# Transposing the normalised attention output by the DMA crossbar instead of by TensorE, per head pair

## The chip, the cores and the metric

The kernel runs on one NeuronCore of a Trainium2 chip. The core has a matmul engine (TensorE, PE in the profile, with its weight loads listed as PEld), a vector engine (VectorE, DVE), an activation engine (ScalarE, ACT), GpSimd (POOL) and a queue engine (SyncE, SP). POOL and SP issue the DMA transfers of this kernel. The metric is the device time of one launch in microseconds. The profile comes from one execution; its times count from the first instruction.

## The reference

Block-sparse attention over 4 batches, 8 heads, 768 positions and a head size of 64, and then a gated feed-forward network (FFN) over the 3072 tokens:

```
scores = (1/8) * q @ k.T                 # per batch and head, 768 x 768
scores = where(mask, scores, -1e9)       # blocks of 32: neighbours, first, last, 3 sampled per row block
attn   = softmax(scores)
x      = (attn @ v), heads side by side  # 3072 x 512
gate   = sigmoid(x @ w_gate);  val = x @ w_val      # 512 -> 1536
out    = (gate * val) @ w_out                       # 1536 -> 512
```

## The kernel before

The work is cut into twelve units, a batch and a third of its queries (256 positions) each; three units make a batch. In a unit the eight heads go as four head pairs, called pair 0 to pair 3. For a pair, three steps of score matmuls (`qk`, L406) fill two PSUM score buffers in turn, ACT takes the exponential (L416), DVE multiplies by the mask (L422), and 24 matmuls (`pv`, L445) form the attention output with one extra column for the softmax sum. `norm` (L453 to L462) takes the reciprocal of that column and multiplies, and writes the tile `x16`: 128 positions in partitions, two halves of 128 features.

The FFN wants features in partitions, so x must be turned into x^T. `turn` (L464) does this by two TensorE transposes per pair into PSUM (L466), and `evac` (L472) copies the result into the tile `xT` on DVE (through L227) or ACT (L225). When all four pairs of a unit are in `xT`, the unit's FFN can start: twelve blocks of eight matmuls (L532), each followed by a tanh on ACT (L543) and a gate on DVE (L548), and at last two output projections of twelve matmuls (`y`, L571), whose results go out by a store from SP's queue (L589).

Two units overlap. In the slots of unit n, the FFN of unit n-1 runs, and in the first two slots the output projections of unit n-2. The values of pair 3 of unit n-1 come in slot 0 of unit n, and the FFN of unit n-1 begins in slot 2.

For batches 1 to 3, q and k are already transposed by the DMA crossbar in the kernel before: one transfer for k and one for q per batch on SP's queue (L375), each of 24 blocks of 128x128. For batch 1, DVE first pairs the heads up (L364). For batches 2 and 3, POOL loads the pairs directly (L622). Batch 0 is transposed on TensorE.

The order of the work on every engine is fixed before the launch by a planner in the kernel, the class `Plan`. Each task has costs in microseconds per engine, dependencies, sometimes a due time, and a lag until its successors may start. The planner runs through time, gives each free engine the first ready task of its list, and so writes one order per engine. The engines then follow that order and wait for each other by semaphores. A DMA task has a lag that stands for its landing: 10 us for the q and k transposes, 55 us for the loads of batches 2 and 3. SP takes its transfers strictly in the written order.

Of the kernel before, what the change touches and what calls it, by code (L numbers as in the profile page):

```python
# [13 lines left out]
f16 = mybir.dt.float16  # L14
# [6 lines left out]
B, H, S, D = 4, 8, 768, 64  # L21
# [3 lines left out]
NP = H // 2  # L25
# [5 lines left out]
UQ = 256  # L31
NU = S // UQ
PE, ACT, DVE, DMA = "PE", "ACT", "DVE", "DMA"
DMA_RATE = 0.385
XB, PB, VB = 4, 4, 5
# [86 lines left out]
def kernel(  # L122
# [11 lines left out]
    nc = tc.nc  # L134
# [6 lines left out]
            name=nc.get_next_instruction_name(), act_func_set_id=_set_id  # L141
# [12 lines left out]
    work = ctx.enter_context(tc.tile_pool(name="work", bufs=1))  # L154
# [90 lines left out]
    plan = Plan({'m': 4, 's': 2})  # L245
# [4 lines left out]
    used = {nm: [] for nm in ("pr", "P", "x16", "th", "ht", "xT")}  # L250

    def ring(nm, bufs):

        i = len(used[nm]) - bufs
        return [used[nm][i]] if i >= 0 else []
# [115 lines left out]
    def xbar(src, dst, b, deps):  # L371


        def go(eng):
            nc.sync.dma_start_transpose(  # L375
                dst[b % 2].rearrange("a p (t n) -> a (p t) n", n=128),
                src.rearrange("a p t h d -> a (p t h d)"),
            )

        return plan.add([(DMA, 0.01)], go, deps, lag=10.0)  # L380
# [48 lines left out]
    class Pair:  # L429
# [23 lines left out]
        def norm(self, eng):  # L453
            rz = work.tile([128, 2, 2, 1], f32, tag="rz", bufs=3, name="rz")
            nc.vector.reciprocal(rz, self.acc[:, :, :, D : D + 1])  # L455
            self.x16 = work.tile([128, 2, 2, D], f16, tag="x16", bufs=4, name="x16")
            nc.vector.tensor_tensor(  # L457
                self.x16,
                self.acc[:, :, :, 0:D],
                rz.broadcast_to([128, 2, 2, D]),  # L460
                op=ALU.mult,
            )  # L462
# [16 lines left out]
        def value(self):  # L479
            a = plan.add([(PE, 0.8)], self.pv, self.products + [vdone[self.b, self.p]],  # L480
                         take=[self.bank])
            used["P"].append(a)
            read["pv", self.b, self.p] = [a]
            self.normed = plan.add([(DVE, 0.6)], self.norm, [a] + ring("x16", 4),
                                   free=[self.bank])

        def xt(self):
            c = plan.add([(PE, 0.12)], self.turn, [self.normed], take=[self.bank2])
            used["x16"].append(c)
            deps = [used["xT"][self.n - XB]] if self.n >= XB else []  # L490
            xdone[self.n].append(
                plan.add([(DVE, 0.29), (ACT, 0.37)], self.evac, [c] + deps,
                         free=[self.bank2])
            )
# [107 lines left out]
    xTs = [[] for _ in units]  # L602
    xdone = [[] for _ in units]
# [171 lines left out]
```

The softmax here doesn't subtract the row's maximum and nothing guards it: scores larger than these inputs give would overflow.

## Time and profile before

| | |
|---|---|
| median of 8 runs | 306.28 us (305.92 to 307.78) |
| the profiled execution | 306.2 us, its span 304.4 us |
| granted TensorE clock | 0.997 |
| PE, DVE, ACT busy | 96%, 66%, 69% of the span |
| transposes of x on PE (L466) | 96, in 48 pairs |
| evacuations of x^T | 31 on DVE (mean 292 ns), 17 on ACT (mean 372 ns) |
| SP's transfers | 24 stores, 6 transposes of q and k, 4 loads of constants |

A row of the groups names line, engine, operation and tiles, then the count, the total busy time, the mean duration, and the idle time of the engine before it with what ended it. Matmul durations overlap, so the place a matmul takes is read from start to start. A row of the timeline has its start and length in microseconds. A row of SP's timeline shows how long the queue was held by issuing the transfer, or by the waits between merged ones, and not when the data landed; the median time to landing stands in the list of DMA issues.

### The profile page before, as it was taken

Reading aid. Unit: us, or ns where it says so; the run is one execution under the profiler, and the core shown is the slowest. Engines: PE = TensorE matmul, PEld = TensorE weight load, DVE = VectorE, ACT = ScalarE, POOL = GpSimd, SP = SyncE. Lnnn points to the kernel's source line nnn. Section 1 sums busy time; section 2 is a strip of 40 time slices with the busy share of each in tenths; the row PEclk is TensorE's granted clock in tenths of the full one; section 3 lists DMA queues with packets and bytes.
Section 4 is the critical chain, followed back from the end, with each engine's and each line's share of the span. In section 5 each row is a group of like instructions: output and inputs, shape, how many; then the busy total and the mean of one; then the engine's idle time right before and its main releaser. Section 6 shows DMA issues by size and latency. Waiting matters only on the chain.

```text
span 304.4 us, 7858 instructions
## 1 busy us (share of the span) xinstructions
PE 291.5 (96%) x3326; PEld 209.7 (69%) x3326; DVE 201.0 (66%) x474; ACT 210.7 (69%) x340; POOL 48.5 (16%) x65
## 2 busy tenths in 40 slices
PE   3978999999999999999999999999999999999994
PEld 1354785786786786786686686687687687687771
DVE  4769878876676678676676577576576577576240
ACT  3669986776776776776776776776776776774431
POOL 8943000584000059200000000000000000000000
PEclk9999999999999999999999999999999999999998
DMA  7999999999500699930100480100100100100101
GB/s 100 179 202 202 206 204 185 234 160 129 121 1 2 158 151 128 156 71 2 71 2 0 129 152 1 71 2 2 69 2 2 69 2 4 69 2 2 69 2 70
DMA packets 62768, 25.75 MB, mean 85 GB/s; under 512 B 45812, under 2 KB 59660, under 8 KB 62732
## 3 DMA queue, kind: packets, MB, share of 16 engines
q0 software_dynamic: 40400, 14.16, 40.9%
q1 hardware_dynamic: 22332, 11.09, 14.7%
q8 instruction: 26, 0.43, 0.6%
q14 instruction: 10, 0.08, 0.1%
HBM read 28.39 MB, written 6.29 MB: 114 GB/s over the span
## 4 chain that ended last, share of the span: by engine, by line
PE 92%; ACT 2%; DMA 2%; POOL 1%; DVE 1%; issue 1%; DVEq 0%; POOLq 0%
PE m L532 42%; PE m L571 21%; PE m L445 13%; PE s L406 13%; DMA k<-in_k_dram 2%; PE m L466 2%; ACT pt L416 1%; PE m L338 1%; ACT mask L225 1%; POOL k L178 1%; POOL q L178 0%; POOL v L178 0%; DVE pt L422 0%; DVE kT L227 0%; PE m L303 0%
## 5 line engine op out<-in xcount | busy, mean ns | idle before, releaser
L416 ACT ACTIVATE pt<-s 128x1024 f16<-128x1024 f32 x144 | 140.2, 1027 | 4.5 <-PE s L406 3.7
L422 DVE TENSOR_TENSOR pt<-pt,mask 128x1024 f16<-128x1024 f16 x144 | 97.2, 687 | 38.9 <-ACT pt L416 38.5
L532 PE MATMUL m<-xT,wg 128*128 128x256 f16 x576 | 86.7, 273 | 0.0
L532 PE MATMUL m<-xT,wv 128*128 128x256 f16 x576 | 86.4, 273 | 0.0
L543 ACT ACTIVATE th<-m 128x256 f32<-128x256 f32 x144 | 54.6, 390 | 43.9 <-PE m L532 36.6
L548 DVE SCALAR_TENSOR_TENSOR ht<-th,m 128x256 f16<-128x256 f32 x144 | 57.3, 417 | 16.2 <-ACT th L543 14.8
L571 PE MATMUL m<-wo,ht 128*128 128x512 f16 x288 | 66.0, 379 | 0.0
L532 PEld LDWEIGHTS <-wv 128*128 128x128 f16 x576 | 56.4, 98 | 6.5
L532 PEld LDWEIGHTS <-wg 128*128 128x128 f16 x576 | 51.3, 98 | 12.5 <-issue 7.2
L445 PE MATMUL m<-vex,pt 128*128 128x65 f16 x1152 | 46.5, 196 | 1.8 <-ACT mask L225 1.6
L445 PEld LDWEIGHTS <-pt 128*128 128x128 f16 x1152 | 42.6, 99 | 7.6 <-issue 5.3
L571 PEld LDWEIGHTS <-ht 128*128 128x128 f16 x288 | 26.6, 98 | 30.7 <-issue 2.1
L406 PE MATMUL s<-qT,kT 64*128 64x256 f16 x576 | 47.1, 279 | 0.6 <-DVE qT L227 0.3
L582 ACT ACTIVATE ysb<-m 128x512 f32<-128x512 f32 x24 | 14.3, 597 | 35.3 <-PE m L571 35.3
L406 PEld LDWEIGHTS <-kT 64*128 64x128 f16 x576 | 22.0, 95 | 15.8 <-issue 8.6
L622 POOL DMA_DIRECT2D kp<-in_k_dram x16 | 13.0, 820 | 63.9 <-DMA kT<-kp 38.2
L455 DVE RECIPROCAL rz<-m 128x4 f32<-128x4 f32 x48 | 8.7, 182 | 19.5 <-PE m L445 18.9
L457 DVE TENSOR_TENSOR x<-m,rz 128x256 f16<-128x256 f32 x48 | 20.4, 425 | 1.7
L227 DVE COPY xT<-m 128x256 f16<-128x256 f16 x31 | 9.0, 292 | 10.9 <-PE m L466 10.9
L466 PE MATMUL m<-ident,x 128*128 128x128 f16 x96 | 13.3, 221 | 0.1
L622 POOL DMA_DIRECT2D qp<-in_q_dram x16 | 13.1, 823 | 1.2 <-DMA kp<-in_k_dram 0.9
L466 PEld LDWEIGHTS <-x 128*128 128x128 f16 x96 | 9.0, 99 | 6.1 <-DVE x L457 0.7
(36 smaller groups left out, 73.2 us busy)
## 6 DMA issues: line engine op xcount, KB each, us to landing
out_dram<-ysb SPq DMA_DIRECT2D x24, 256.0 KB, 2.0
v<-in_v_dram POOLq DMA_DIRECT2D x3, 768.0 KB, 11.1
wg<-in_moe_w_gate_dram POOLq DMA_DIRECT2D x4, 384.0 KB, 12.7
wv<-in_moe_w_val_dram POOLq DMA_DIRECT2D x4, 384.0 KB, 13.7
wo<-in_moe_w_out_dram POOLq DMA_DIRECT2D x3, 512.0 KB, 16.9
kp<-in_k_dram POOLq DMA_DIRECT2D x16, 96.0 KB, 4.7
qp<-in_q_dram POOLq DMA_DIRECT2D x16, 96.0 KB, 4.4
k<-in_k_dram POOLq DMA_DIRECT2D x4, 192.0 KB, 5.4
```

The costliest lines, as they stand in the source:

```text
L406: nc.tensor.matmul(score[self.bank.slot][:, a, i, :], kT[b % 2][o : o + D, p, t * 128 : (t + 1) * 128], qT[b % 2][o : o + D, p, u * UQ : ( ...
L416: nc.scalar.activation(self.pt, score[self.bank.slot], AF.Exp, bias=0.0, scale=SCALE)
L422: nc.vector.tensor_tensor(self.pt, self.pt, m.unsqueeze(1).broadcast_to([128, 2, 2, UQ]), op=ALU.mult,)
L445: nc.tensor.matmul(self.acc[:, s, a, :], self.steps[t // 2].pt[:, a, t % 2, s * 128 : (s + 1) * 128], vex[self.b % 2][:, 2 * self.p + a, t ...
L457: nc.vector.tensor_tensor(self.x16, self.acc[:, :, :, 0:D], rz.broadcast_to([128, 2, 2, D]), op=ALU.mult,)
L466: nc.tensor.transpose(m16(self.bank2.slot)[:, s * 128 : (s + 1) * 128], self.x16[:, s, :, :], ident,)
L532: nc.tensor.matmul(pg[:, i, :], w[:, c, f * 128 : (f + 1) * 128], xTs[self.n][0][:, c, :], start=(c == 0), stop=(c == 3),)
L543: nc.scalar.activation(th, spare[bank.slot][:, 0:UQ], AF.Tanh, bias=0.0, scale=0.5)
L548: nc.vector.scalar_tensor_tensor(self.ht[:, f, :], in0=box[0], scalar=1.0, in1=spare[bank.slot][:, UQ : 2 * UQ], op0=ALU.add, op1=ALU.mult,)
L571: nc.tensor.matmul(spare[bank.slot], self.ht[:, f, s * 128 : (s + 1) * 128], wo[:, f, :], start=(f == 0), stop=(f == NF - 1),)
L582: nc.scalar.activation(ysb, spare[bank.slot], AF.Copy, bias=0.0, scale=0.5)
L622: nc.gpsimd.dma_start(dst[:, p, :, a, :], src[b, 2 * p + a].rearrange("(n t) d -> n t d", t=NT),)
```

## The change

For units 1 to 11, the two transposes on TensorE and the copy out of PSUM are replaced by one crossbar transfer per head pair, issued from SP's queue: `x16` (128 x 256) goes as two 128x128 blocks straight into the pair's place in `xT`. The planner gives it 0.05 us of its DMA resource and a lag of 3.0 us. The ring of `x16` tiles grows from four to six, as a tile is now held until its transfer has read it. Unit 0 keeps the TensorE path. The transposes of q and k stay as they were.

```diff
         def norm(self, eng):
...
-            self.x16 = work.tile([128, 2, 2, D], f16, tag="x16", bufs=4, name="x16")
+            self.x16 = work.tile([128, 2, 2, D], f16, tag="x16", bufs=6, name="x16")
...
-            self.normed = plan.add([(DVE, 0.6)], self.norm, [a] + ring("x16", 4),
+            self.normed = plan.add([(DVE, 0.6)], self.norm, [a] + ring("x16", 6),
                                    free=[self.bank])
 
+        def xbar(self, eng):
+            if not xTs[self.n]:
+                xTs[self.n].append(
+                    work.tile([128, NP, UQ], f16, tag="xT", bufs=XB, name="xT")
+                )
+            nc.sync.dma_start_transpose(
+                xTs[self.n][0][:, self.p, :].rearrange("a (s n) -> a s n", s=2),
+                self.x16.rearrange("a s h d -> a (s h d)"),
+            )
+
         def xt(self):
+            if self.n > 0:
+                deps = [used["xT"][self.n - XB]] if self.n >= XB else []
+                c = plan.add([(DMA, 0.05)], self.xbar, [self.normed] + deps, lag=3.0)
+                used["x16"].append(c)
+                xdone[self.n].append(c)
+                return
             c = plan.add([(PE, 0.12)], self.turn, [self.normed], take=[self.bank2])
```

## The prediction

> **What bounds the kernel now.** I read the engine shares and the slices first, then the chain, then a window of one unit, then the timeline of PE, and last the queue of SP, which takes on the new work.
>
> ```profile
> PE 291.5 (96%) x3326; PEld 209.7 (69%) x3326; DVE 201.0 (66%) x474; ACT 210.7 (69%) x340; POOL 48.5 (16%) x65
> ...
> PE 92%; ACT 2%; DMA 2%; POOL 1%; DVE 1%; issue 1%; DVEq 0%; POOLq 0%
> ...
> L457 DVE TENSOR_TENSOR x<-m,rz 128x256 f16<-128x256 f32 x48 | 20.4, 425 | 1.7
> L227 DVE COPY xT<-m 128x256 f16<-128x256 f16 x31 | 9.0, 292 | 10.9 <-PE m L466 10.9
> L466 PE MATMUL m<-ident,x 128*128 128x128 f16 x96 | 13.3, 221 | 0.1
> ...
> out_dram<-ysb SPq DMA_DIRECT2D x24, 256.0 KB, 2.0
> ...
> kT<-kp SPq DMA_TRANSPOSE x3, 7.2
> qT<-qp SPq DMA_TRANSPOSE x3, 5.7
> ```
>
> PE is the bound and almost the whole chain. DVE and ACT have 30% to spare. The window of one whole unit (columns: PE, PEld, DVE, ACT, POOL busy, then granted clock) confirms it: PE is busy from end to end at full clock, and from 36 to 300 us the wait view has no row for PE's matmuls.
>
> ```profile
> 148.32:171.40 23.08, 23.08 (x277) 16.95 (x274) 15.44 (x35) 16.78 (x28) 0.00 (x0) 1.00 0.07 25
> ```
>
> So what leaves PE is gained in full, and whatever PE waits for is lost in full. The timeline of PE (start, length) shows what a pair of transposes costs in place, first without one, then with one:
>
> ```profile
> 150.56 0.60 PE L532 MATMUL m<-xT,wv 128*128 128x256 f16 x4
> 151.09 0.28 PE L406 MATMUL s<-qT,kT 64*128 64x256 f16 x2
> ...
> 157.98 0.60 PE L532 MATMUL m<-xT,wv 128*128 128x256 f16 x4
> 158.42 0.27 PE L466 MATMUL m<-ident,x 128*128 128x128 f16 x2
> 158.63 0.50 PE L406 MATMUL s<-qT,kT 64*128 64x256 f16 x6
> ```
>
> From the FFN's four to the scores is 0.53 us without and 0.65 us with the transposes. Durations of 221 ns overlap; scores after an FFN or output matmul pay a switch of about 0.1 us, which the shorter transposes partly cover. Unrounded start times give 0.112 us for a pair of transposes in front of scores, and 0.111 in front of an output projection.
>
> **Part 1: transposes leave PE.** 44 head pairs (units 1 to 11), 0.112 us each: 4.9 us off PE, 0.45 us per unit. All of it lies on the path. The 44 PSUM evacuations (0.29 us on DVE or 0.37 on ACT) lie beside PE; they are worth nothing, and should PE not be the bound they would be 1.5 us per unit at most. The deeper ring of x16 and the PSUM slots that come free cost nothing; the wait of norm on the sixth last crossbar transfer is over by then, as six pairs are one and a half units, 34 us.
>
> The Trainium skill, page "VectorE: DVE Perf Modes", section "The three transpose paths", puts a 128x128 transpose at 390 ns on TensorE and 1309 ns by the crossbar, and its rules advise TensorE where PSUM will do, which speaks against this change. By its figures the sum would be 88 x 0.39 = 34 us off PE and a transfer of 2.6 us; the trace's 0.112 us for two decides.
>
> **Part 2: 44 crossbar transfers on SP's queue.** No row shows one of two blocks. The rows of 24 blocks: SP is held 3.58 to 4.25 us (5.62 once, under loads), about 0.15 us a block, and landing follows the end of issue by 1.5 to 3.6 us (5.50 minus 3.58, 6.12 minus 3.96, 5.74 minus 4.25, 7.24 minus 3.65). A plain store holds SP 0.33 us and lands after 2.0 us, 5.8 to 7.5 us while batch loads run. So one transfer takes 0.33 plus 1.5 to 3.6, or 1.8 to 3.9 us; I take 2.3, near the quiet rows. The ends are 1.8 and 7.8 (the slowest row of 24 blocks). SP's total, 44 x 0.4 = 18 us, is no bound.
>
> What waits: the FFN of a unit needs all four pairs, and the last, pair 3, has least time. From the end of its norm to the first FFN matmul the timeline gives 6.63 us in seven units, 5.15 in units 1 and 7, 4.43 in unit 4, 4.45 in unit 11; between them lie pair 0's values, two scores and two output projections. With two transposes gone from that stretch, 0.22 less: 4.2 us at the worst. 2.3 us fits, and so does 3.9. The new waits on PE's queue (at most four semaphores at 51 ns, 11 times) run ahead of the matmuls: the one of scores at 68.41 us was over 1.9 us before they began.
>
> **Part 3: the queue in front of it.** SP issues in order:
>
> ```profile
> 48.57 5.62 SPq L375 DMA_TRANSPOSE kT<-kp  x1
> 54.24 0.58 SPq L589 DMA_DIRECT2D out_dram<-ysb  x1
> 54.87 4.04 SPq L375 DMA_TRANSPOSE qT<-qp  x1
> 58.95 0.63 SPq L589 DMA_DIRECT2D out_dram<-ysb  x1
> ```
>
> The store at 54.24 had its data at 52.04 (the ysb row of ACT) and stood 2.2 us behind kT; the next was ready at 55.27 and stood 3.7 us behind qT. A pair 3 caught there keeps PE waiting. Three places:
>
> Unit 1: norm ends 50.85, inside kT's issue. Issue at 54.2, landing 56.5; the FFN would start at 56.01 less four pairs, 55.56. Loss 1.0 us. Its ends: 0 if it goes first; 7.6 us if qT goes first too (that lands at 62.65, plus some 0.5).
>
> Units 4 and 7: kT and qT of batches 2 and 3 are entered when the planner's clock says so, at 10 plus 55 us of its lags after the last batch's qT, however early the data land. Its costs for a unit are 12 x 0.88 + 2 x 2.6 + 6 x 0.54 + 4 x 0.8 = 22.20 us without transposes, where the trace has 23.09. So 65.02 planned us are 67.6 of the trace's: from 52.3 (q's pair copies, started at 50.77 and worth 1.5) plus 0.25 (two transposes gone before a fixed due time) to 120.2, then 187.8. Norms of pairs 2 and 3 end at 115.48 and 120.85 in unit 4, at 186.62 and 189.41 in unit 7. Both marks fall between, 0.7 and 1.6 us ahead of pair 3, which is no more than this reckoning's error. If caught: SP has nothing else to wait for, issues kT and qT after pair 2, and is free after 0.4 + 3.65 + 0.3 + 4.25 (unit 4) or 0.4 + 3.96 + 0.3 + 3.58 (unit 7), at 124.1 and 194.9. Landing 126.4 and 197.2 against FFN starts of 125.07 and 194.35: 1.3 and 2.8 us. Lower ends 0; upper ends 1.6 us more by the 3.9.
>
> In unit 4, POOL's batch loads follow kT's landing (38.2 us of POOL's wait is on it) and come 6 to 18 us later than before; batch 3 is used 70 us on, so that costs nothing. Output stores queued behind cost nothing either: four ysb buffers, and the last store has no crossbar near.
>
> **The sum.** The profiled execution took 306.2 us (span 304.4 and 1.8 around it), 0.1 under the median. 306.2 - 4.9 + 1.0 + 2.0 (one of the two later places, near the mean of 1.3 and 2.8) = 304.3; on the median, 304.4.
>
> **Rivals.** *Caught in neither later place:* DVE has fewer copies, so norm may come earlier than its old place behind v's copies; against it, both marks lie ahead of pair 3. 306.3 - 4.9 + 1.0 = 302.4, 301.4 without unit 1's loss.
>
> *Caught in both:* 306.3 - 4.9 + 1.0 + 1.3 + 2.8 = 306.5, no difference. For it: both marks fall inside; against: one error shifts both.
>
> *Slower, by latency:* a two-block transfer takes as long to land as one of 24. It decides at 5.8 us, where units 1, 4, 7 and 11 lose 0.9 + 1.6 + 0.9 + 1.6 = 5.0 us. At kT's 7.2 us the seven other units lose 0.8 each and these 2.3, 3.0, 2.3, 3.0: 16 us, 317. For it: no landing under 5.5 in the transposes' rows, and 7.5 for a store under loads; against: issue grows with blocks, and the stores' 2.0.
>
> *Slower, by order:* in unit 1 qT enters before pair 3, 7.6 us in place of 1.0, about 309 to 311. Against: DVE's order has norm (50.22) just before q's copies (50.77), qT needs the last of four, and norm only moves earlier.
>
> **How the numbers follow.** Forecast 0.38; neither 0.20; both 0.20; latency 0.11; order 0.06; 0.05 for a rearranged plan that loses more. Measurement can tell about 0.2%, 0.6 us. The forecast's own range is 303 to 306. Low is the neither case without unit 1's loss, 301.4; high takes in both with slower landing (306.5 plus 1.6), 308.1; what is left out is most of latency and order. Faster: 0.36 of the forecast, 0.20, 0.04 of both, 0.02 of a mild latency: 0.62. Same: 0.11 of both, 0.02 and 0.01: 0.14. Slower: 0.24.
>
> **What would show it.** Right: no transpose on L466 after unit 0; units without kT and qT at 22.64 us with PE full; two-block transfers landing in about 2.3 us; a PE wait on xT's DMA only at the FFN's start in units 1 and 4 or 7, with the transfer's issue late behind qT. Wrong: a PE wait at every unit's FFN (latency), units still at 23.09 (the pair costs less than 0.112 once gone), or one wait of 5 us or more in unit 1 (order).

## The result, and the profile after

The changed kernel is slower by about 1%: 309.49 us median of 11 runs (307.09 to 310.42) against 306.42 us for the kernel before in 32 runs. The ratio on record, which is not that of the two medians (1.0100), is 1.0081, 95% interval 1.0062 to 1.0101. The forecast was 304.4 us. The profiled execution took 308.3 us, its span is 306.5 us.

The page's rows that answer to those of before:

```profile
PE 288.6 (94%) x3238; PEld 202.7 (66%) x3238; DVE 192.4 (63%) x444; ACT 205.9 (67%) x326; POOL 48.5 (16%) x65
...
PE   3978999699999999999999999699999999999995
...
PEclk9999999999999999999999999899999999999999
...
PE 76%; DMA 18%; POOL 2%; issue 1%; ACT 1%; DVE 0%; POOLq 0%
...
L548 PE MATMUL m<-xT,wg 128*128 128x256 f16 x576 | 87.8, 274 | 5.3 <-DMA xT<-x 5.3
```

The rows of slices of before:

```profile
PE   3978999999999999999999999999999999999994
...
PEclk9999999999999999999999999999999999999998
```

PE has less to do, as intended: 88 transposes and their weight loads are gone. But PE's row of slices, which was full from unit 1 to the end, has two notches (a 6 in the eighth and in the 26th slice). DMA has gone from 2% to 18% of the chain: 4% are transfers of x^T, and most of the rest are the first loads, to which the profile follows the chain back from unit 1's wait. (It links them by copies on DVE that end as the late transfer is issued; the rows of SP's queue below show what held that transfer.) And the FFN's first matmuls, L548 in the new file, have 5.3 us of idle time in front of them, in three waits that each end with a crossbar transfer. The granted clock has a notch too, in the slice of PE's second one.

The starts of the units' FFNs say where the time went. In the quiet units, from one FFN to the next is 22.64 us (103.62, 126.27, 148.92, 171.56, 194.20), where before it was 23.09. That is the 0.45 us that four pairs of transposes were to save. Three stretches are longer: from unit 1's FFN to unit 2's 25.23 us (2.6 too many), from unit 2's to unit 3's 23.25 (0.6), from unit 7's to unit 8's 26.81 (4.2). The timeline of PE at units 1 and 7 (start, length, idle before and what ended it):

```profile
55.14 0.50 PE L548 MATMUL m<-xT,wg 128*128 128x256 f16 x3
58.07 0.27 PE L548 MATMUL m<-xT,wg 128*128 128x256 f16 x1 [2.42 <-DMA xT<-x]
...
194.20 0.50 PE L548 MATMUL m<-xT,wg 128*128 128x256 f16 x3
197.14 0.36 PE L548 MATMUL m<-xT,wg 128*128 128x256 f16 x1 [2.44 <-DMA xT<-x]
```

Three matmuls run, on pairs 0 to 2; the fourth needs pair 3 and waits. From the first start to the fourth are 2.93 and 2.94 us, where three matmuls take 0.33: 2.6 us lost each time. SP's queue at the same places shows why:

```profile
46.38 1.17 SPq L492 DMA_TRANSPOSE xT<-x  x1
48.72 6.92 SPq L375 DMA_TRANSPOSE kT<-kp  x1
55.76 1.18 SPq L492 DMA_TRANSPOSE xT<-x  x1
...
185.43 1.38 SPq L492 DMA_TRANSPOSE xT<-x  x1
187.16 3.60 SPq L375 DMA_TRANSPOSE kT<-kp  x1
191.06 3.63 SPq L375 DMA_TRANSPOSE qT<-qp  x1
194.79 1.20 SPq L492 DMA_TRANSPOSE xT<-x  x1
```

Pair 3's norm had ended at 51.00 and 188.57 us, but its transfer was issued at 55.76 and 194.79, when SP came free of k, and of k and q. Once issued it landed in 2.27 us in unit 1, and PE went on 2.35 us after the issue in unit 7. The columns of the next view are PE, PEld, DVE, ACT and POOL busy, and then the granted clock; the two windows are unit 7's wait and the time just after it:

```profile
194.20:197.20 3.00, 0.56 (x6) 0.36 (x5) 0.69 (x1) 1.99 (x3) 0.00 (x0) 1.00 0.79 155
197.20:200.60 3.40, 3.40 (x35) 2.78 (x35) 0.85 (x3) 0.38 (x1) 0.00 (x0) 0.50 0.42 151
```

After the wait, PE works for 3.4 us at half clock. The 24 value matmuls that take 0.78 us elsewhere took 1.34 us there. That is the rest of what unit 7 lost, 4.2 us: 2.6 of waiting and 1.6 for the clock. After unit 1's wait the clock did not fall in this execution.

The books close to 0.1 us. Up to the last copy of the output out of PSUM (300.08 before, 302.87 after) the trace is 2.8 us longer: minus 4.9 for 44 pairs, plus 2.6 (unit 1), 0.6 (unit 2), 2.6 and 1.6 (unit 7), and 0.4 by which unit 0's FFN started later (31.64 against 31.27), before the change has begun to act. From that copy to the end of the span are 3.66 us, 0.7 less than the 4.35 of before; the traces of the other runs with 44 transfers have 3.65 to 3.69, and no run here shows why.

### The profile page after: what moved, and what is told of

Its sections match the earlier page's. It is cut to its first block, busy times and chain, and to the rows that moved or that the text cites. A ratio compares the mean times of both kernels' runs of the same rounds, so it can differ in the third digit from the quotient of the medians.

```text
span 306.5 us, 7750 instructions
## 1 busy us (share of the span) xinstructions
PE 288.6 (94%) x3238; PEld 202.7 (66%) x3238; DVE 192.4 (63%) x444; ACT 205.9 (67%) x326; POOL 48.5 (16%) x65
## 4 chain that ended last, share of the span: by engine, by line
PE 76%; DMA 18%; POOL 2%; issue 1%; ACT 1%; DVE 0%; POOLq 0%
PE m L548 39%; PE m L587 17%; PE m L445 11%; DMA v<-in_v_dram 10%; PE s L406 10%; DMA wv<-in_moe_w_val_dram 5%; DMA xT<-x 4%; POOL q L178 1%; POOL k L178 0%; POOL wv L188 0%; POOL wg L188 0%; ACT ysb L598 0%; POOL v L178 0%; DVE vex L384 0%; ACT pt L416 0%
## 5 line engine op out<-in xcount | busy, mean ns | idle before, releaser
L548 PE MATMUL m<-xT,wg 128*128 128x256 f16 x576 | 87.8, 274 | 5.3 <-DMA xT<-x 5.3
L548 PE MATMUL m<-xT,wv 128*128 128x256 f16 x576 | 87.0, 274 | 0.0
L564 DVE SCALAR_TENSOR_TENSOR ht<-th,m 128x256 f16<-128x256 f32 x144 | 56.5, 417 | 20.2 <-ACT th L559 19.9
L548 PEld LDWEIGHTS <-wv 128*128 128x128 f16 x576 | 56.6, 98 | 12.6 <-issue 5.8
L548 PEld LDWEIGHTS <-wg 128*128 128x128 f16 x576 | 50.6, 98 | 14.5 <-issue 9.3
L445 PEld LDWEIGHTS <-pt 128*128 128x128 f16 x1152 | 44.1, 100 | 5.8 <-issue 4.7
L384 DVE COPY vex<-v 128x768 f16<-128x768 f16 x16 | 5.1, 369 | 3.3 <-DMA v<-in_v_dram 3.3
L338 PE MATMUL m<-ident,pr 128*128 128x128 f16 x48 | 5.8, 276 | 0.7 <-DVE pr L329 0.4
L338 PEld LDWEIGHTS <-pr 128*128 128x128 f16 x48 | 4.1, 125 | 3.0 <-DVE pr L329 1.7
```

What stands on the lines that cost most here:

```text
L338: nc.tensor.transpose(m16(bank.slot)[:, (t - t0) * 128 : (t - t0 + 1) * 128], box[0][:, t, :, :], ident,)
L445: nc.tensor.matmul(self.acc[:, s, a, :], self.steps[t // 2].pt[:, a, t % 2, s * 128 : (s + 1) * 128], vex[self.b % 2][:, 2 * self.p + a, t ...
L548: nc.tensor.matmul(pg[:, i, :], w[:, c, f * 128 : (f + 1) * 128], xTs[self.n][0][:, c, :], start=(c == 0), stop=(c == 3),)
L564: nc.vector.scalar_tensor_tensor(self.ht[:, f, :], in0=box[0], scalar=1.0, in1=spare[bank.slot][:, UQ : 2 * UQ], op0=ALU.add, op1=ALU.mult,)
```

## The experiments

The theory after the result: pair 3's transfer stands on SP's queue behind the long transposes of k and q, in units 1 and 7; PE waits 2.6 us each time, and such a wait can drop the clock to half for 3.4 us. The first rival: small crossbar transfers are slow among other DMA traffic wherever they stand, or SP's traffic slows PE. The second, on the clock: it has another cause than PE's idleness.

### Unit 1's place in the queue alone

The planner gets a due time for k's and q's transposes of batch 1 (and a smaller lag, which keeps the places of batches 2 and 3 where they were). PE's order is that of the changed kernel.

```
-        return plan.add([(DMA, 0.01)], go, deps, lag=10.0)
+        return plan.add([(DMA, 0.01)], go, deps, at=52.0 if b == 1 else 0.0, lag=10.0)
...
-                lag=55.0,
+                lag=54.2,
```

> Only unit 1's queue order changes: the crossbar transfer of k for batch 1 gets a due time of 52 us in the plan, so that pair 3 of unit 1 stands in front of it on SP's queue; all other entries of SP's queue keep their places and PE's order is the same to the last instruction. Queue theory: the wait of 2.6 us before unit 1's FFN goes (at most 0.3 us is left), the one of unit 7 stays at 2.6 us, and the time falls by 2.6 us, or by up to 4.3 us where the clock had dropped after it: 305.2 to 307.0 against 309.5 for the changed kernel. Rival (small crossbar transfers are slow among other DMA traffic, wherever they stand): the landing time stays long, the wait moves by less than 0.7 us, and the time stays at 308.8 to 310.

Measured: 304.85 us median (303.29 to 305.79), ratio to the kernel before 0.9925 (0.9891 to 0.9959). The wait view of PE from 36 us on has one row and one wait left, unit 7's:

```profile
PE m L548 <- DMA xT<-x: 2.6, 1, 2.6
```

One place on a queue turns the sign of the whole change. The gain is a little over the range that was written down; in the profiled execution unit 2 lost 0.16 us in place of 0.6.

### Unit 7's place alone

```
-                lag=55.0,
+                lag=56.0,
```

> Only the lag of batch loads in the plan is 56 us in place of 55, which puts pair 3 of unit 7 in front of k and q of batch 3 on SP's queue, and one output store of unit 4 in front of k of batch 2; unit 1 is as it was. Queue theory: the wait of 2.6 us before unit 7's FFN goes, the one of unit 1 stays, and the half clock of 3.4 us that followed unit 7's wait goes too: 305.2 to 307.0, the same gain as from unit 1 alone within 1.5 us. Rival (latency among other traffic): 308.8 to 310.

Measured: 305.06 us (304.15 to 306.2), just under the range, ratio 0.9951 (0.9921 to 0.998). Unit 7's wait is gone, unit 1's is there (three matmuls from 54.96 us, the fourth at 57.99, 2.7 us lost) and unit 2's too (0.5 us):

```profile
PE m L548 <- DMA xT<-x: 2.9, 2, 2.5
```

Against the changed kernel's ratio of 1.0081, unit 1's place is worth 0.0156 (4.8 us) and unit 7's 0.0130 (4.0 us): more than a wait of 2.6 us each, by about what a half clock costs. With one of the two waits left, the clock was at 0.994 in five of the ten runs of this section and the one before, and at 0.999 or over in the others.

### Both places

The due time of 52 us, and a lag of 60 us:

```
-        return plan.add([(DMA, 0.01)], go, deps, lag=10.0)
+        return plan.add([(DMA, 0.01)], go, deps, at=52.0 if b == 1 else 0.0, lag=10.0)
...
-                lag=55.0,
+                lag=60.0,
```

> Both queue places are mended (the due time of 52 us for batch 1, a lag of 60 us for the batch loads), all 44 crossbar transfers stay. Queue theory: of the waits only the 0.6 us before unit 2's FFN is left, which comes from the batch loads; 306.4 minus 4.9 for the transposes plus 0.6 makes 302.1, range 301.2 to 303.2, and the granted clock is as in the kernel before, 0.997 or over, in every run. Rival (latency, or SP's extra traffic slowing PE): 307.5 to 310, since no work is taken away.

Measured: 300.94 us (300.87 to 301.37), ratio 0.981 (0.9796 to 0.9825). No FFN waits on x^T. The singles add up: 0.0156 and 0.0130 make 0.0286, the two together give 0.0271. All 44 transfers are still there, so neither their number nor their own latency made the kernel slow, and the first rival falls. (PE's order changed in this run, which it did not in the two singles; the next run keeps it.) It was 1.2 us better than the sum I had written, 0.6 of it unit 2's wait, which did not come: pair 3 landed 5.32 us after its issue there, 0.3 us before the FFN began. The other 0.6 stay open. The longer lag overdid it for batch 3, whose q came late for one group of scores:

```profile
PE s L406 <- DMA qT<-qp: 0.7, 1, 0.7
```

### The better version: the due time alone

With the due time and the lag of 55 us as it was, the planner's clock moves by itself far enough that unit 7 is mended as well.

```
-        return plan.add([(DMA, 0.01)], go, deps, lag=10.0)
+        return plan.add([(DMA, 0.01)], go, deps, at=52.0 if b == 1 else 0.0, lag=10.0)
```

> The due time of 52 us for k and q of batch 1 alone, with the lag of 55 us kept: by the plan this puts pair 3 in front of k in unit 1 and also in unit 7, and leaves PE's order as in the changed kernel. Queue theory: no wait of PE on x^T in units 1 and 7, and none of 0.7 us on q of batch 3 as with the lag of 60 us; at most the 0.6 us of unit 2: 300.3 to 301.5 against 306.4 to 306.9 for the kernel before, a ratio of 0.979 to 0.983. Rival (the gain of the run with both places mended came from its changed PE order, not from the queue): 303 or more.

Measured: 301.52 us (300.56 to 302.43), ratio 0.9847 (0.9823 to 0.9872), with PE's order the same as in the changed kernel. Time and ratio lie just above the ranges written down: units 1 and 2 still lose 0.4 and 0.3 us from start to start, as their pair 3 took 4.83 and 6.22 us to land. SP's queue at unit 1 (compare the rows above), and PE's waits from 36 us on:

```profile
46.11 5.82 SPq L492 DMA_TRANSPOSE xT<-x  x2
52.04 1.19 SPq L605 DMA_DIRECT2D out_dram<-ysb  x1
53.28 4.25 SPq L375 DMA_TRANSPOSE kT<-kp  x1
57.64 3.60 SPq L375 DMA_TRANSPOSE qT<-qp  x1
...
PE m L548 <- DMA xT<-x: 0.4, 2, 0.2
```

The two transfers of x^T now stand in front; the 5.82 us are the time between them, with pair 3 issued at 50.76. This version and the one before it both beat the kernel before and the changed one; their intervals meet, and which of the two is better was not settled.

### A wait made where there was none

The due time stays, which mends unit 1; a lag of 52 us puts k and q of batch 2 in front of pair 3 of unit 4.

```
-        return plan.add([(DMA, 0.01)], go, deps, lag=10.0)
+        return plan.add([(DMA, 0.01)], go, deps, at=52.0 if b == 1 else 0.0, lag=10.0)
...
-                lag=55.0,
+                lag=52.0,
```

> The opposite test: the due time of 52 us mends unit 1, and a lag of 52 us in place of 55 puts k and q of batch 2 in front of pair 3 of unit 4, which stood in front of them in the changed kernel and cost nothing there. In unit 7 pairs 2 and 3 both come after k and q, early enough not to matter. Queue theory: a new wait of PE before unit 4's FFN of 2.5 to 5 us (pair 3 is issued about 9 us after its data are there, and lands beside the batch loads that k's landing starts), with or without 1.7 us for the clock after it; unit 1 and 7 without one: 303 to 307. Rival (units 1 and 7 are slow for another reason than their place in the queue): unit 4 has no wait, and the time is that of the run with the due time alone, 300.3 to 301.5.

Measured: 308.81 us (308.55 to 310.7), ratio 1.0102 (1.0072 to 1.0132). The sign and the place are as expected; the price is higher than the range written down. Unit 1 kept a wait of 0.4 us. SP's queue, then the timeline of PE, then two windows (PE, PEld, DVE, ACT, POOL busy, clock):

```profile
115.47 4.29 SPq L375 DMA_TRANSPOSE kT<-kp  x1
120.05 3.68 SPq L375 DMA_TRANSPOSE qT<-qp  x1
123.83 1.20 SPq L492 DMA_TRANSPOSE xT<-x  x1
...
129.02 0.37 PE L548 MATMUL m<-xT,wg 128*128 128x256 f16 x1 [5.82 <-DMA xT<-x]
...
126.50:129.00 2.50, 0.00 (x0) 0.00 (x0) 0.00 (x0) 0.00 (x0) 2.50 (x4) 0.51 1.89 192
129.00:133.40 4.40, 4.38 (x39) 3.45 (x39) 1.54 (x4) 0.41 (x2) 4.11 (x6) 0.50 2.12 198
```

Issued 6.8 us after its norm (117.08), pair 3 needed another 5.15 us to land, beside batch 3's loads, which POOL had begun at 122.33 when k landed. From unit 4's FFN to unit 5's are 30.63 us, 8.0 over 22.64: 6.0 of waiting and 2.0 from a half clock that lasted 6.8 us, 4.4 of them while PE worked. Against the run with the due time alone, which differs from this one in the lag only, the ratio is 0.0255 higher, or 7.8 us, so that is the whole difference. One caught pair 3 costs about as much here as two did in the changed kernel.

### The waits filled with useless work

PE's and SP's order stay as in the changed kernel; in front of the FFNs of units 1 and 7 twelve matmuls are added, weights times weights, into the bank that the FFN then overwrites.

```
+                if f == 0 and self.n in (1, 7):
+                    for i in range(NF):
+                        nc.tensor.matmul(
+                            spare[bank.slot],
+                            wo[:, i, 0:128],
+                            wo[:, i, :],
+                            start=(i == 0),
+                            stop=(i == NF - 1),
+                        )
```

> The order of the changed kernel is kept, but in front of the FFN of units 1 and 7 PE gets twelve useless matmuls of 512 columns (weights times weights, into the bank that the FFN then overwrites), 12 x 0.216 = 2.6 us each, which fill the two waits. Clock theory (an idle PE of 2.6 us can cost a half clock of 3.4 us, 1.7 us of time, on top of the wait): 5.2 us of work are added and nothing gets slower; the clock is 0.997 or over in all runs, and the time is that of the undisturbed runs of the changed kernel, 306.8 to 307.8, below its median of 309.5. Rival (the clock has another cause, or PE was not waiting there): 309.5 plus up to 5.2, so 309.5 to 314.7.

Measured: 307.29 us (306.37 to 308.29), ratio 1.0011 (0.9996 to 1.0026). The granted clock was 0.998 or over in all ten runs. In the changed kernel it was 0.994 or lower in ten of twelve (the record has the span and clock of one run, of 307.41 us, that is not in the median):

```
changed kernel, span in us by mean granted clock:
1.000         305.6  305.3
0.994         306.5  306.2  305.7  307.9
0.988, 0.989  308.2  308.0  308.6  307.7  308.0  307.4
```

The stretch after unit 7's wait lasted 3.413 us by the trace's record of the clock. At half clock that is 1.7 us, or 0.0056 of the span; the steps of the mean clock are one and two such stretches. The timeline at unit 1 shows the useless matmuls in the place of the wait:

```profile
55.02 2.76 PE L547 MATMUL m<-wo 128*128 128x512 f16 x12
57.62 0.77 PE L557 MATMUL m<-xT,wg 128*128 128x256 f16 x4
58.22 0.60 PE L557 MATMUL m<-xT,wv 128*128 128x256 f16 x4
```

5.2 us of work were added, and the kernel became 0.7% faster than the changed one (1.0011 against 1.0081). The clock fell because PE stood idle, and this makes up the distance from about 307.2 to 309.5 us. What is left over the forecast is the waits themselves, unit 2's among them. Unit 2's wait was 1.57 us in this execution, as its pair 3 took 7.62 us to land, and the clock did not fall there.

### Half of the filling

Six matmuls in each place instead of twelve; against the run before:

```
-                    for i in range(NF):
+                    for i in range(6):
...
-                            stop=(i == NF - 1),
+                            stop=(i == 5),
```

> As the run with twelve useless matmuls per caught unit, with six of them (1.3 us), so that half of the wait is left, 1.3 us in units 1 and 7. If the clock falls only after a longer idle stretch: the same time as with twelve, 306.8 to 307.8, clock 0.997 or over. If any wait can drop it: 308 to 310, with clocks of 0.989 to 0.994 in a good part of the runs.

Measured: 307.51 us (306.55 to 308.51), ratio 1.0038 (1.001 to 1.0066). Neither expectation holds cleanly: the clock was 1.000 in four of six runs, 0.992 and 0.994 in two. In the profiled one, a wait of 1.93 us in unit 1 was followed by 3.4 us at half clock (from 59.18 us), and one of 0.99 us in unit 7 was not. So a wait of 1.9 us can drop the clock; here it fell in two of six runs, with the longer waits of the changed kernel in ten of twelve.

The ten traces on record say more than the lengths of the waits do. In each, the stretches at one clock in the trace's record are whole numbers of steps of 3.413 us, except the last, which the end of the run breaks off: 82 in the kernel before, 51, 1 and 31 in the changed one, 11, 1 and 71 here. Laid over PE's idle time, these steps sort all the cases. Half clock came after every step in which PE was idle for 1.93 us or more, and after none with 1.59 us or less. In the changed kernel unit 7's wait lies whole in the step that ends at 197.18 us, and the clock fell there; unit 1's is split at 57.24 us into 1.59 and 0.83, and the clock held. The 2.53 us of the run with unit 7's place mended are split into 1.46 and 1.07, and the clock held too. The steps lie elsewhere in every execution, which would be why the same wait costs more in some runs than in others. This was read from the traces afterwards; no run was made to test it.

### Pair 3 on TensorE throughout

```
-            if self.n > 0:
+            if self.n > 0 and self.p < 3:
```

> Pair 3 of every unit stays on TensorE, pairs 0 to 2 of units 1 to 11 go by the crossbar, the queue's due times are as in the changed kernel. Theory: only pair 3 has little time before its FFN, so no FFN waits on a transfer; 33 pairs leave PE, 33 x 0.112 = 3.7 us, and the time is 306.5 - 3.7 = 302.8, range 302.0 to 303.6, the clock at 0.997 or over. Rival (pair 2, caught behind k and q too, or the batch loads, still make PE wait): 304 to 307.

Measured: 302.37 us (301.57 to 303.08), ratio 0.9878 (0.9854 to 0.9902). No wait of PE from 30 us on, and 33 pairs at 0.112 us give the 302.8 us expected, within the spread. Other pairs stand behind k and q too, and it costs nothing: pair 0 of unit 2 had its norm at 56.83 us and was issued at 60.96. Only pair 3 was short of time.

## Why the prediction was wrong, point by point

**Transposes leave PE, 4.9 us: right.** The quiet units went from 23.09 to 22.64 us, the very number given.

**Landing of a small transfer, 2.3 us: right in the quiet, wrong under loads.** Outside the loads, 14 of the 20 transfers whose landing is recorded in the changed kernel's trace took 2.27 to 2.32 us, the others 2.4 to 3.7. While loads ran they took 5.2 to 8.5 us there, and 4.7 to 8.8 over all runs. I had rows for that (a store's 5.8 to 7.5 us, the 7.8 of a transpose) and kept the 7.8 as an end of the range, without asking which unit's pair 3 falls into a load. Unit 2's does: issued at 74.78, landed after 6.50 us, 0.6 us lost. Part of it is the time that was left: I gave the quiet units 6.63 less 0.22 us, and the trace has 5.62, since the new plan puts pair 0's values (0.78 us) behind the first FFN block.

**SP's hold per transfer, 0.33 us: wrong, without consequence.** It is 1.17 us for two blocks in most rows, 2.28 at most; the 0.15 us a block read from transposes of 24 would have given 0.3.

**Unit 1, loss of 1.0 us: the mechanism right, the term mis-sized, 2.6 us.** The issue came at 55.76 and not at 54.2, because k's transpose held SP for 6.92 us where it had held it for 5.62 before; the FFN was ready at 55.14 and not at 55.56, for the reason just given; the landing was as taken. Against this, the first three matmuls, 0.33 us, did not have to wait for pair 3.

**Units 4 and 7, one of the two caught: right in number, and in where the risk was.** The reckoning with the planner's clock put both marks between pairs 2 and 3; unit 7 was caught and cost 2.6 us of waiting against 2.8 forecast, unit 4 escaped. That it was one of the two is in part luck, since both marks lay ahead of pair 3 by no more than the reckoning's own error. The forced catch of unit 4 cost 6.0 us of waiting, not the 1.3 that the step gave. For 2.9 us of this I wrote that the loads that follow k's landing cost nothing, and forgot that pair 3 lands among them (5.15 us in place of 2.3); the rest is that the forced order put k further ahead, so that pair 3 was issued 6.8 us after its norm and not 3.3.

**The step that failed the forecast: "whatever PE waits for is lost in full".** It is lost, and more. The sum had no term for the clock. A wait of 2.6 us costs up to 1.7 us on top, and in half of the changed kernel's runs it did so twice. With the terms as measured, 306.3 - 4.9 + 2.6 + 2.6 + 0.6 makes 307.2 us with the clock full, near what the two runs at full clock took (307.1 and 307.4); with two stretches at half clock it makes 310.6, near the slowest run of 310.4. So of the 5.1 us between the forecast and the median, 2.8 are waits that were too small in the sum (1.6 for unit 1, 0.6 for unit 7, 0.6 for unit 2, which it did not have), and about 2.3 are the clock, which it put at nothing. The clock stood at 1.00 in each window that I read, and none of them had a wait in it, so they said nothing of what a wait does. But a row was in reach: the clock's row of before ends in an 8. There PE's last matmul ends at 300.04 us, and from 302.55 on the clock is at half.

**The rivals.** "Caught in both" (306.5) came nearer to the time than the forecast did, but by luck: unit 1's 2.6 us and the clock made it up, and unit 4 was not caught. "Caught in neither" fell with unit 7, and "order" with unit 1, where q was issued after pair 3. The latency rival was wrong for the quiet units and right in a small way for unit 2. The Trainium skill (page "VectorE: DVE Perf Modes", section "The three transpose paths") puts a 128x128 transpose on TensorE at 390 ns, which gave an estimate of 34 us; the runs show 4.9. The page's advice to transpose on TensorE where PSUM will do does not hold here once the queue is in order (a ratio of 0.9847).

## What to carry to other kernels

A transfer is worth its place on the queue, not its own latency: before a short, urgent transfer is put on a queue that also carries long ones, look at what stands in front of it at every point of the run, and give the long ones a due time at which nothing urgent follows. On a kernel whose PE is never idle, price each new wait of PE at its length plus a possible stretch at reduced clock, and judge the time that is left by the slowest landing of a comparable transfer under the loads of that moment.

## What the runs showed of the hardware that was not expected

- A crossbar transpose of two 128x128 blocks holds SP for 1.17 us in most rows and lands, in the quiet, mostly in 2.27 to 2.32 us; one of 24 blocks holds it for 3.6 to 6.9 us. From the shortest of each (1.17 and 3.60 us), an estimate: about 0.1 us a block, and 0.95 us that do not shrink with the blocks.
- An idle stretch of TensorE of 1.9 to 2.6 us can be followed by 3.4 us at half clock, in some executions and not in others; in one of 5.8 us the clock fell before its end, to 6.8 us at half. Useless matmuls in the idle stretch prevented it. In the ten traces it goes by the idle time within one step of 3.413 us: 1.93 us and more dropped the clock, 1.59 us and less did not.
- Beside batch 2's loads issued by POOL, the same small transfer took 4.7 to 8.8 us to land in unit 2 over all runs, two to four times its quiet time.
